# Retention and a two-expert router on one core: short pieces on two column halves, expert 5 turned by transfers, and two constants of the planner

## The chip, the cores and the metric

The kernel runs on one core of a Trainium2 chip. The core has five instruction streams: TensorE (PE, with its weight loads shown apart as PEld), VectorE (DVE), ScalarE (ACT), GpSimd (POOL) and SyncE (SP), and 16 DMA engines that all of them share. SP and POOL issue nearly all transfers. Each stream runs its instructions in the order in which the program has them. The metric is the device time of one execution in microseconds (us). A profiled execution also gives its span, which is the time from its first to its last instruction.

## The reference

Eight batches of 576 tokens go through retention with 8 heads of 64 columns, and the result, as 4608 rows of 512, through a mixture of 8 experts of which each row takes two.

```python
scores = scale * np.matmul(q, k.transpose(0, 1, 3, 2))
Dmat = np.where(rel >= 0, gamma[:, None, None] ** rel[None, :, :], 0.0)
attn = np.matmul(scores * Dmat, v)
x = np.ascontiguousarray(attn.transpose(0, 2, 1, 3)).reshape(B * S, H * D)
...
noisy_logits = x @ w_gate + np.log1p(np.exp(x @ w_noise)) * noise
top2 = np.argpartition(-noisy_logits, 2, axis=1)[:, :2]
top2_w = softmax of the two logits
...
for e in range(8):
    for k in range(2):
        mask = top2[:, k] == e
        h = np.maximum(x[mask] @ w1[e], 0.0)         # 512 -> 1024
        out[mask] += top2_w[mask, k, None] * (h @ w2[e])   # 1024 -> 512
```

The softmax line is told in words; the other lines are the reference's, shortened.

## The kernel before

**Planner.** The kernel first records its operations (`Plan.op`), each with an engine or a choice of engines, a cost, a priority, the buffers that it reads and writes and, for transfers, the DMA time `dma`. `Plan.run` then takes the operations one by one, always the one that can start first by its own bookkeeping, and writes them out in that order. So the costs decide nothing but order, the choice between two engines, and buffer numbers; what waits for what on the chip follows from the data. SP's and POOL's transfers have a lane each, in which a transfer may not be planned ahead of the eighth before it. A POOL transfer was counted as `dma / 0.85`, and one over 2 (the casting weight transfers, 2.9) also pushed back the finish of SP's last eight.

**First stage.** Retention works in 16 units: a pair of batches (`bp`, four of them), four of the eight heads (`hq`), one batch of the pair. Per unit SP loads k, q and v (`load`), the values are scaled and cast to bf16 (`cast`, on ACT, DVE or POOL), PE transposes K and Q (`tr`, line 482) and forms the masked scores (`scores`, 507), the states (`states`, 540) and the output (`out_`, 575 and 585). The last 64 tokens of a batch go through `tail`. The attention's PE work is done on parts of the array: the trace names the part, for example 64\*64 or 128\*64 (rows\*columns). After four units, `route` does a batch pair: logits, the two largest, ranks within each expert (`ranks`, 752 and 754), a table of row numbers by expert (`table`, 805), and the rows themselves, transposed back (828), evicted into `xg` buffers (276 on ACT, 278 on DVE), joined with their weights (834 on POOL) and written to DRAM as `xd` (837 on SP). The room for these rows is ten `xg` buffers, so a pair's rows wait until those of the pair before have landed in `xd`.

**Experts.** An expert has up to 1216 rows, in ten pieces: nine of 128 rows and one of 64, the short piece (`size`). A tile is two to four pieces of one expert (`tiles`), 29 tiles in all, numbered t0 to t28. t0 to t8 belong to experts 0 to 2 and take rows that were routed by the first three batch pairs; they run between and behind the attention's work (`up`, line 1037, then `down`, 1114). The other twenty, from t9 on, go one after another: `wide` (1063) multiplies by `w1`, 32 matmuls per tile with as many columns as the tile has rows, and PE interleaves them with the second multiplication (`second`, 1114) of the tile before, eight matmuls of 128x512 per piece. For a short piece the same eight matmuls are used, and 64 of the 128 result rows are ignored. The very last tile's second multiplication stands alone at the end of `record` (planned at line 1247; its matmuls show as 1114).

Rows are fetched two tiles ahead by gathers on POOL (`fetch`, 961), at the pace of PE: each waits for a matmul that the plan had just emitted. Then they are turned: by PE (983) and an eviction for experts 0 to 5, by transposing transfers on SP (973) for experts 6 and 7 (`CROSS = 6`). A piece in which both kinds of choices meet needs four small operations on DVE (1001 to 1007, `gm` and `im`), which wait for the gather.

Weights of experts 0 to 2 come by casting transfers on POOL (894, 898: four transfers of 512 KB each for an expert), planned behind the loads of units 10, 15 and 15 (`WAIT`). The others come by SP (908, 911) and are cast by ACT and DVE (276, 278), when the tile that frees their room begins.

**Results.** `finish` scales a piece's result by its weight. For a row's first expert it goes to DRAM as `yd` (1148 or 1150, then 1154 on SP). For its second expert `prev` gathers the first result from `yd` (1129 on POOL), DVE joins both (1158), and POOL scatters the rows to the output (1162). Near the end POOL gets a drain (1250), planned behind the first scatter of the last tile but two. After the planned part a loop for overflowing experts (line 1263) runs zero times here.

The functions that the change touches, with the lines of the profile:

Of the kernel before, what the change touches and what calls it, by code (L numbers as in the profile page):

```python
# [10 lines left out]
BF16 = mybir.dt.bfloat16  # L11
# [19 lines left out]
WAIT = (10, 15, 15)  # L31
CROSS = 6
# [7 lines left out]
HD = 64  # L40
C9 = 9
# [14 lines left out]
class Plan:  # L56
# [55 lines left out]
    def run(self):  # L112
# [35 lines left out]
        while ready:  # L148
            pick = None
            for o in ready:  # L150
# [22 lines left out]
                for e, c in o.eng.items():  # L173
# [3 lines left out]
                    if o.dma and len(lanes[e]) >= 8:  # L177
                        t = max(t, lanes[e][-8].fin)
# [20 lines left out]
            if o.dma:  # L199
# [42 lines left out]
class Kernel:  # L242
# [807 lines left out]
    def wide(self, i, t, prio, g2=None):  # L1050
# [5 lines left out]
        for f in range(KF):  # L1056
            p = self.psum("exp")

            def pe(_, f=f, p=p):
# [21 lines left out]
    def down(self, i, t):  # L1081
# [6 lines left out]
        part = lambda g: [divmod(x, KF) for x in range(g * m, g * m + m)]  # L1088

        class Down:  # L1090
# [5 lines left out]
            @staticmethod  # L1096
            def deps(g):
                return ([(hT[f // (KF // len(hT))], f if len(hT) == 4 else f // 2) for s, f in part(g)] +
                        [(w, KD + f // 2) for s, f in part(g)], [po[s] for s in sorted({s for s, f in part(g)})],
                        0.216 * m)  # L1100

            @staticmethod
            def ends(g):
                return [s for s, f in part(g) if f == KF - 1]
# [3 lines left out]
    def second(self, e, po, hT, c, f):  # L1108

# [5 lines left out]
                                        start=(f == 0), stop=(f == KF - 1))  # L1115

# [17 lines left out]
    def finish(self, i, t, s, prio):  # L1134
# [8 lines left out]
        if k != "S":  # L1143
            y = pl.buf("half", "exp")

            def ev(eng, y=y, po=po, g=g, n=n):
                if eng == "ACT":
                    nc.scalar.activation(y.t[:n], po.t[:n], Act.Copy, scale=g()[:n])  # L1148
                else:
                    nc.vector.tensor_scalar(y.t[:n], po.t[:n], g()[:n], None, Alu.mult)  # L1150
            pl.op({"ACT": 0.69, "DVE": 0.7}, 0, ev, r=[po] + src, w=[y], prio=prio)
# [4 lines left out]
        if k != "F":  # L1156
            o, b = pl.buf("half", "exp"), d["prv"][s]
            pl.op("DVE", 0.75, lambda _, o=o, b=b, po=po, g=g, n=n: nc.vector.scalar_tensor_tensor(  # L1158
                o.t[:n], po.t[:n], g()[:n], b.t[:n], Alu.mult, Alu.add), r=[po, b] + src, w=[o], prio=prio)
# [12 lines left out]
    def record(self):  # L1172
# [42 lines left out]
        for i, t in enumerate(ts[:ne]):  # L1215
# [6 lines left out]
            for k in range(KF):  # L1222
                r, w, c = g.deps(k)
                pl.op("PE", c, lambda _, g=g, k=k: [0 for _ in g(k)], r=r, w=w, prio=pr)
# [187 lines left out]
```

## Time and profile before

| what | value |
|---|---|
| median of three runs | 440.3 us (438.19 to 440.85) |
| the profiled execution | 441.0 us, span 439.4 us |
| granted TensorE clock, mean | 0.954 |
| PE, PEld busy | 385.7 us (88%), 245.4 us (56%) |
| DVE, ACT, POOL busy | 179.7 (41%), 240.0 (55%), 286.3 us (65%) |
| second multiplications (1114) | 608 matmuls of 128x512, 202.8 us |
| first multiplications of the wide tiles (1063) | 636 matmuls, 189.0 us |
| PE transposes of gathered rows (983) | 216 of 128x128, 15.4 us |
| transposing transfers on SP (973) | 20, median 4.5 us to landing |
| casting weight transfers on POOL | 12 of 512 KB, median 10.5 us to landing |

The busy share of PE is a mean over two stages. Up to about 186 us the attention, the routing and the first nine tiles share all engines; from there to 431.6 us the wide tiles run. Matmuls overlap in the pipeline, so the mean duration of one (383 ns for 128x512) is longer than its distance to the next. In a row of the windows the columns are: stretch, its length, then busy time and instructions of PE, PEld, DVE, ACT and POOL, then the mean granted clock, the share of the DMA engines' time and GB/s. In a row of the timeline they are: start, duration, engine, line, operation, tiles, form and count, and in brackets how long the engine sat idle before it and what ended that. The form named is that of the first instruction of the row.

### The profile page before, as it was taken

Reading aid. Unit: us, or ns where it says so; the run is one execution under the profiler, and the core shown is the slowest. Engines: PE = TensorE matmul, PEld = TensorE weight load, DVE = VectorE, ACT = ScalarE, POOL = GpSimd, SP = SyncE. Lnnn points to the kernel's source line nnn. Section 1 sums busy time; section 2 is a strip of 40 time slices with the busy share of each in tenths; the row PEclk is TensorE's granted clock in tenths of the full one; section 3 lists DMA queues with packets and bytes.
Section 4 is the critical chain, followed back from the end, with each engine's and each line's share of the span. In section 5 each row is a group of like instructions: output and inputs, shape, how many; then the busy total and the mean of one; then the engine's idle time right before and its main releaser. Section 6 shows DMA issues by size and latency. Waiting matters only on the chain. (4 is left out here: it accounts for less than half of the span.)

```text
span 439.4 us, 11080 instructions
## 1 busy us (share of the span) xinstructions
PE 385.7 (88%) x4252; PEld 245.4 (56%) x4288; DVE 179.7 (41%) x489; ACT 240.0 (55%) x398; POOL 286.3 (65%) x355
## 2 busy tenths in 40 slices
PE   1787884889898959899979999999999999999992
PEld 1665774777676746575545545555454454454451
DVE  2544388778378278213043334026025031131221
ACT  3589693866787436466554747446536524424320
POOL 8875678997789337553446566566577677567344
PEclk9999597969899969999999999999999999999998
DMA  7999999999999988448399897895799997645323
GB/s 193 276 309 233 291 240 310 318 212 247 314 263 196 227 168 242 118 137 297 116 325 387 261 382 236 276 383 167 251 352 278 292 212 224 187 157 174 121 78 140
DMA packets 102489, 105.34 MB, mean 240 GB/s; under 512 B 31870, under 2 KB 80511, under 8 KB 102434
## 3 DMA queue, kind: packets, MB, share of 16 engines
q1 hardware_dynamic: 87170, 67.72, 51.3%
q0 software_dynamic: 15264, 36.89, 32.7%
q8 instruction: 34, 0.56, 0.5%
q14 instruction: 21, 0.17, 0.1%
HBM read 83.20 MB, written 26.63 MB: 250 GB/s over the span
## 5 line engine op out<-in xcount | busy, mean ns | idle before, releaser
L1114 PE MATMUL ps<-W,half 128*128 128x512 bf16 x608 | 202.8, 383 | 0.7 <-issue 0.2
L1063 PE MATMUL ps<-big,W 128*128 128x512 bf16 (+4 forms) x636 | 189.0, 330 | 4.0 <-DVE half L1048 2.8
L1046 ACT ACTIVATE half<-ps 128x512 bf16<-128x512 f32 (+5 forms) x179 | 90.2, 506 | 117.6 <-PE ps L1063 100.7
L961 POOL DMA_INDIRECT xg<-xd,xi x80 | 83.1, 1039 | 64.6 <-ACT half L1046 20.5
L1114 PEld LDWEIGHTS <-half 128*128 128x128 bf16 x640 | 62.6, 99 | 72.6 <-issue 5.6
L1063 PEld LDWEIGHTS <-W 128*128 128x128 bf16 x640 | 63.0, 98 | 47.6 <-issue 0.3
L1158 DVE SCALAR_TENSOR_TENSOR half<-ps,xg,half 128x512 f32<-128x512 f32 (+1 forms) x39 | 29.2, 749 | 79.9 <-PE ps L1114 68.6
L1162 POOL DMA_INDIRECT out_dram<-half,xg x39 | 38.8, 995 | 26.3 <-issue 12.5
L515 DVE TENSOR_TENSOR half<-ps,mask 128x512 bf16<-128x512 f32 x64 | 40.0, 683 | 20.2 <-PE ps L507 20.0
L1129 POOL DMA_INDIRECT half<-yd,xg x39 | 39.4, 1011 | 11.9 <-issue 10.4
L276 ACT ACTIVATE half<-ps 128x1024 bf16<-128x1024 bf16 (+1 forms) x33 | 32.7, 1010 | 12.1 <-PE ps L482 9.4
L482 PE MATMUL ps<-ident__69,half 128*128 128x128 bf16 x256 | 23.8, 251 | 16.6 <-ACT half L449 9.1
L457 POOL TENSOR_TENSOR half<-big,tab 128x1024 bf16<-128x1024 f32 x15 | 28.6, 1904 | 10.3 <-DMA big<-in_q_dram 10.3
L1037 PE MATMUL ps<-half,W 128*128 128x256 bf16 (+1 forms) x288 | 29.8, 260 | 4.5 <-ACT half L276 2.8
L464 POOL TENSOR_TENSOR half<-big,tab 128x512 bf16<-128x512 f32 x32 | 33.0, 1046 | 0.0
L1148 ACT ACTIVATE half<-ps,xg 128x512 f32<-128x512 f32 (+1 forms) x32 | 21.8, 685 | 16.1 <-PE ps L1114 15.8
L482 PEld LDWEIGHTS <-half 128*128 128x128 bf16 x256 | 18.6, 114 | 19.5 <-ACT half L449 9.6
L1037 PEld LDWEIGHTS <-W 128*128 128x128 bf16 x288 | 24.6, 100 | 8.2 <-issue 3.8
L276 ACT ACTIVATE tb<-ps 64x512 bf16<-64x512 f32 x32 | 18.9, 590 | 13.5 <-PE ps L540 13.3
L276 ACT ACTIVATE W<-big 128x1024 bf16<-128x1024 f32 x21 | 21.4, 1055 | 5.7 <-DMA big<-in_moe_w_dram 5.5
L276 ACT ACTIVATE xT<-ps 128x512 bf16<-128x512 f32 (+1 forms) x40 | 19.9, 556 | 7.2 <-PE ps L656 5.0
L1158 DVE SCALAR_TENSOR_TENSOR half<-ps,gm,half 128x512 f32<-128x512 f32 x6 | 4.5, 751 | 46.9 <-ACT half L1148 39.8
(170 smaller groups left out, 415.7 us busy)
## 6 DMA issues: line engine op xcount, KB each, us to landing
big<-in_moe_w_dram SPq DMA_DIRECT2D x40, 512.0 KB, 8.9
yd<-half SPq DMA_DIRECT2D x41, 256.0 KB, 5.2
big<-in_k_dram SPq DMA_DIRECT2D x32, 256.0 KB, 6.1
big<-in_q_dram SPq DMA_DIRECT2D x16, 512.0 KB, 6.0
big<-in_v_dram SPq DMA_DIRECT2D x32, 256.0 KB, 6.3
W<-in_moe_w_dram POOLq DMA_DIRECT2D x12, 512.0 KB, 10.5
xd<-xg SPq DMA_DIRECT2D x16, 264.0 KB, 5.0
xg<-xd,xi POOLq DMA_INDIRECT x80, 4.4
```

Source lines behind the costliest of these rows:

```text
L276: self.nc.scalar.activation(out, in_, Act.Copy)
L464: self.eng(e).tensor_tensor(o, i, t, Alu.mult)
L482: nc.tensor.transpose(v[:, hp, x, :], i[:, y, hp * P:(hp + 1) * P], ident.t)
L515: nc.vector.tensor_tensor(S.t.bitcast(BF16).rearrange("p (h c x) -> p h c x", h=2, c=2)[:, h], p[h].t.rearrange("p (c x) -> p c x", c=2), ...
L961: ins = nc.gpsimd.indirect_dma_start(out=x.t[:n, :], out_offset=None, in_=self.xd[:rows, :], in_offset=IOff(ap=xi.t[:n, h:h + 1], axis=0), ...
L1037: nc.tensor.matmul(pv()[:, f2, :], lhsT=w.t[:, o:o + P], rhs=xv()[:, di, :n], start=(di == 0), stop=(di == KD - 1))
L1046: self.nc.scalar.activation(o, i, Act.Relu)
L1063: self.mm = nc.tensor.matmul(p.t[:, :n], lhsT=w.t[:, o:o + P], rhs=xv()[:, di, :n], start=(di == 0), stop=(di == KD - 1))
L1114: self.mm = self.nc.tensor.matmul(po.t, lhsT=hv[:, c:c + P], rhs=self.W[e].t[:, o:o + DM], start=(f == 0), stop=(f == KF - 1))
L1129: pl.op("POOL", 1.3, lambda _, b=b, iy=iy, n=self.size(j): nc.gpsimd.indirect_dma_start(out=b.t[:n, :], out_offset=None, in_=self.yd[:rows ...
L1158: pl.op("DVE", 0.75, lambda _, o=o, b=b, po=po, g=g, n=n: nc.vector.scalar_tensor_tensor(o.t[:n], po.t[:n], g()[:n], b.t[:n], Alu.mult, Al ...
L1162: ins = nc.gpsimd.indirect_dma_start(out=self.out[:, :], out_offset=IOff(ap=io()[:n], axis=0), in_=o.t[:n, :], in_offset=None, bounds_chec ...
```

## The change

There are four edits, and what the planner makes of them.

1. **Short pieces.** In `down`, a short piece no longer takes part in the interleaving. Its second multiplication stands by itself behind the last step of the tile that follows, as `halves`: for each of the eight parts of `w2` two matmuls of 256 columns with a 64-column stationary operand, the first into result partitions 0 to 63, the second into 64 to 127. `finish` then evicts the two parts by two instructions (`sums`).
2. **Expert 5** (`CROSS` 6 to 5). Its ten pieces, tiles t20 to t22, are turned by transfers on SP, not by PE.
3. **The planner's lanes.** A POOL transfer is counted as `dma / 0.5`, no longer as `dma / 0.85`, and the push on SP's last eight finishes is gone.
4. **The units behind which weights begin** (`WAIT`): 11, 14, 15, no longer 10, 15, 15.

```diff
-WAIT = (10, 15, 15)
-CROSS = 6
+WAIT = (11, 14, 15)
+CROSS = 5
...
-                        t = max(t, lanes[e][-8].fin)
+                        t = max(t, lanes[e][-8])
...
-                    x += o.dma / 0.85
+                    x += o.dma / 0.5
                     if dma_free.get("SP", 0.0) > t + c:
                         dma_free["SP"] += o.dma
-                        for y in lanes["SP"][-8:] if o.dma > 2 else ():
-                            if y.fin > t + c + self.DMA_LAT:
-                                y.fin += o.dma
...
-                lanes[e].append(o)
+                lanes[e].append(o.fin)
...
                 for _ in it:
                     pass
+                if g2:
+                    g2.rest(f)
...
-        part = lambda g: [divmod(x, KF) for x in range(g * m, g * m + m)]
+        full = [s for s in range(m) if self.size(js[s]) == P]
+        short = [s for s in range(m) if self.size(js[s]) < P]
+        n = len(full)
+        part = lambda g: [(full[x // KF], x % KF) for x in range(g * n, g * n + n)]
+        alone = lambda g: [(s, f) for s in short for f in range(KF)] if g == KF - 1 else []
...
+            def rest(g):
+                for s in short if g == KF - 1 else ():
+                    self.halves(e, po[s], hT, self.off(js)[s])
...
+    def halves(self, e, po, hT, c):
+        k = KF // len(hT)
+        for f in range(KF):
+            hv = hT[f // k].t.bitcast(BF16).rearrange("p (f s) -> p f s", f=k)[:, f % k]
+            o = KD * F + f * DM
+            for y in range(2):
+                self.mm = self.nc.tensor.matmul(po.t[y * HD:(y + 1) * HD, :MIDC], lhsT=hv[:, c:c + HD],
+                                                rhs=self.W[e].t[:, o + y * MIDC:o + (y + 1) * MIDC],
+                                                start=(f == 0), stop=(f == KF - 1), skip_group_check=True)
+    def sums(po, n):
+        return [(slice(0, DM), po.t[:n])] if n == P else [
+            (slice(y * MIDC, (y + 1) * MIDC), po.t[y * HD:(y + 1) * HD, :MIDC]) for y in range(2)]
```

Since the costs changed, the order changed on every engine. Up to about 85 us of the profile the orders are the same. Behind that, these are the moves that the prediction speaks of. On SP, the loads of unit 13 stand ahead of the second pair's row writes (837), which they followed in part, and the loads of unit 14 stand close behind these writes. On POOL, the third and fourth casting transfers of expert 0 come later by some ten instructions; those of expert 1 begin ahead of unit 15's casts, two of expert 2 follow these, then four gathers (t6, t7), the first three small operations of the last routing (731, 744, 760), a third transfer of expert 2, a gather of t8, seven small operations, and the fourth transfer; the four gathers stood behind all of these before. On DVE the third pair's routing up to `MM` stands ahead of unit 14's masks, and the rest of it ahead of unit 15's. On PE t2's first multiplication and the third pair's table stand among unit 15's work, ahead of its tail, and four transposes of t3 to t5 ahead of the last ranks; ten pieces, t9 to t12, are turned in a row ahead of the first wide tile. The gather of t15's second piece follows the fifth group of t10's first multiplications, before the seventh. On SP expert 7's weights stand behind the transposing transfers of t20 to t23. On POOL the drain stands behind the third scatter of tile t26, before it stood behind the second; one scatter of t26, two gathers by `prev` for t28, four scatters of t27 and two of t28 follow it.

More of the change, by code (lines that the diff above doesn't have):

```diff
@@ L40 @@
 HD = 64
+MIDC = DM // 2
 C9 = 9
@@ L1223, in record @@
                 r, w, c = g.deps(k)
-                pl.op("PE", c, lambda _, g=g, k=k: [0 for _ in g(k)], r=r, w=w, prio=pr)
+                pl.op("PE", c, lambda _, g=g, k=k: ([0 for _ in g(k)], g.rest(k)), r=r, w=w, prio=pr)
                 for s in g.ends(k):
@@ L1245, in record, with last @@
                 for s in range(len(po)):
-                    pl.op("PE", 1.74, lambda _, s=s: [self.second(e, po[s], hT, self.off(ts[-1][1])[s], f) for f in range(KF)],
+                    def last(_, s=s):
+                        c = self.off(ts[-1][1])[s]
+                        if self.size(ts[-1][1][s]) < P:
+                            self.halves(e, po[s], hT, c)
+                        else:
+                            for f in range(KF):
+                                self.second(e, po[s], hT, c, f)
+                    pl.op("PE", 1.74 if self.size(ts[-1][1][s]) == P else 0.95, last,
                           r=[(hT[f // 2], f) for f in range(KF)] + [(self.W[e], KD + f) for f in range(4)], w=[po[s]], prio=pr)
```

27 lines of the change are left out of this document (16 added, 11 removed).

## The prediction

> **What bounds the kernel now.** The page's slices first, then the windows of the second half, then PE's waits.
>
> ```profile
> span 439.4 us, 11080 instructions
> ...
> PE   1787884889898959899979999999999999999992
> ...
> DMA  7999999999999988448399897895799997645323
> ```
> ```profile
> 186.00:225.00 39.00, 38.03 (x294) 23.89 (x298) 6.59 (x18) 23.64 (x39) 17.79 (x19) 1.00 0.64 195
> 225.00:235.00 10.00, 7.21 (x37) 4.19 (x38) 3.70 (x12) 4.62 (x8) 4.92 (x5) 0.83 1.01 378
> 235.00:431.60 196.60, 195.45 (x1082) 100.62 (x1102) 56.04 (x91) 92.53 (x165) 125.45 (x124) 1.00 0.77 242
> ```
> ```profile
> PE ps L752 <- DVE MM L724: 6.7, 2, 4.4
> ...
> PE ps L983 <- DMA xg<-xd,xi: 0.6, 1, 0.6
> ```
>
> A slice is 11 us. From the seventeenth on PE is full but for one; ahead of that it has holes, while the DMA engines stand at 8 or 9 nearly all the time. So two stages have different limits. From 235 to 431.6 PE is 99.4% busy at full clock: there only less PE work, or a new wait, moves anything. At 225 to 235 stands one hole. In the first stage PE's longest wait is for the routing (L752). The chain that ended last holds only the last transfer and tells nothing; the timeline shows that the tail hangs on POOL:
>
> ```profile
> 411.74 0.75 DVE L1158 SCALAR_TENSOR_TENSOR half<-ps,xg,half 128x512 f32<-128x512 f32 x1 [2.70 <-PE ps L1114]
> 415.19 0.75 DVE L1158 SCALAR_TENSOR_TENSOR half<-ps,xg,half 128x512 f32<-128x512 f32 x1 [2.70 <-PE ps L1114]
> 413.29 0.99 POOL L1162 DMA_INDIRECT out_dram<-half,xg  x1 [2.96 <-issue]
> 421.95 0.98 POOL L1162 DMA_INDIRECT out_dram<-half,xg  x1 [7.67 <-DVE half L1158]
> 433.57 0.99 POOL L1162 DMA_INDIRECT out_dram<-half,xg  x1 [0.30 <-POOLq L1263]
> 427.77 3.83 PE L1114 MATMUL ps<-W,half 128*128 128x512 bf16 x17
> L1250 POOLq DRAIN  x1: 8001/8001/8001, 413.1 to 413.1; - x1
> ```
>
> PE ends at 431.60. POOL's drain holds its queue to 421.1, and then ten transfers follow, 1.29 us apart without a gap (from 421.95 to 433.57 are nine steps), to 434.56.
>
> **Part 1, short pieces: -4.5 us.** Each expert's last piece has 64 rows. A matmul of 512 columns costs (3.83 - 0.38)/16 = 0.2156 us (the L1114 row, its last one's latency taken off), eight of them 1.72. They become eight pairs of 256 columns, one on each column half. Whether pairs run side by side, the attention shows:
>
> ```profile
> 129.98 0.65 PE L540 MATMUL ps<-half,half 128*64 128x192 bf16 x16
> 130.56 0.44 PE L540 MATMUL ps<-half,half 64*64 64x64 bf16 x16
> ...
> 126.60 1.04 PE L1037 MATMUL ps<-half,W 128*128 128x256 bf16 x8
> 127.57 0.64 PE L507 MATMUL ps<-half,half 64*64 64x128 bf16 x32
> 128.14 1.05 PE L1037 MATMUL ps<-half,W 128*128 128x256 bf16 x8
> ```
>
> The first row holds eight matmuls of 192 and eight of 64 columns on half the array's columns: 2048 columns, 0.86 us one after another at 0.421 ns each. The next row starts after 0.58: two at a time (0.43) and a change of shape. What a change costs: the first L1037 row's 8 x 256 columns take 0.86 and L507 starts after 0.97, so 0.11 going in; 32 x 128 columns, four at a time, take 0.43 and the next row starts after 0.57, so at most 0.14 going out. A short piece then costs 8 x 0.108 + 0.21 = 1.07 and saves 0.65. Seven of the eight stand ahead of the tail: 4.5. The eighth ends PE earlier behind POOL's ten transfers and counts nothing. The pieces' evictions become two instructions each on ACT and DVE, busy for less than half of the time from 235 on; if that cover were gone, each would cost one more start, some tenths of a us.
>
> The Trainium skill, TensorEngine Tiling (Array Packing), Key Properties, speaks against this: changing the tiling mode drains TensorE. The trace agrees that it costs something, the 0.11 and 0.14 above. If such a drain laid bare the latency of the last full matmul too (0.38 less 0.22 of columns, on each side), a piece would save 0.33 and the part 2.3.
>
> **Part 2, expert 5 by transfers: -2.1 us.**
>
> ```profile
> 221.51 1.50 PE L983 MATMUL ps<-ident__69,xg 128*128 128x128 bf16 x24
> 222.85 0.54 PE L1063 MATMUL ps<-big,W 128*128 128x192 bf16 x2
> L973 SPq DMA_TRANSPOSE big<-xg x20: 1172/1224/1697, 333.7 to 376.0; - x20
> ```
>
> 24 transposes move the next start by 1.34 us, 56 ns each; 36 full ones and 4 of half the size go, 2.1 us of PE, and with them five evictions. SP gets ten issues of 1.22 us, and expert 7's weights and some rows of y queue behind them, each behind a transfer that waits for its gather. No engine waited for any of the twenty such transfers before, and the new ones stand as far ahead of their tiles; so nothing, and at worst their own issue time for a tile, 4.9.
>
> **Part 3, order of the wide stage: -4.0 us (0 to -5.2, or +2.5), and +1.0.** The hole at 225:
>
> ```profile
> 218.04 2.06 SPq L911 DMA_DIRECT2D big<-in_moe_w_dram  x4
> 215.93 0.99 POOL L961 DMA_INDIRECT xg<-xd,xi  x1 [0.52 <-ACT half L1046]
> 218.96 1.00 POOL L961 DMA_INDIRECT xg<-xd,xi  x1 [2.03 <-ACT half L1046]
> 226.91 0.16 DVE L1001 TENSOR_TENSOR gm<-xg 128x1 f32<-128x1 f32 x1 [4.27 <-DMA xg<-xd,xi]
> 227.79 0.24 PE L1063 MATMUL ps<-big,W 128*128 128x192 bf16 x1 [2.82 <-DVE half L1048]
> ```
>
> DVE waited for one gather (218.96), issued after weight loads (218.04) had begun and landing 7.9 us later; PE's evictions queued behind it on DVE. The clock in that window, 0.83 over 10 us, is 1.7 more; with 0.65 of wait for another gather (the L983 row) the hole is worth 5.2. In the changed order this gather takes the place that the one before it has now, 215.93, ahead of the loads. But DVE's wait also moves, ahead of an eviction of transposes; if the gather is late nevertheless, the hole grows by up to 2.5. I take -4.0, near the whole, since the place of the gather is what the rows show to matter. On the other side ten pieces are now turned in one row ahead of the first wide tile, with two PSUM buffers for them; PE turns two in 0.45, an eviction takes 0.69 (DVE's copy, below) or more: about 1 us of wait, an estimate.
>
> **Part 4, the first stage: -4 us (-10 to +6).** What it offers:
>
> ```profile
> 100.00:120.00 20.00, 17.81 (x350) 13.62 (x342) 11.73 (x23) 14.54 (x23) 15.13 (x20) 0.91 1.04 282
> 155.00:170.00 15.00, 9.66 (x78) 7.47 (x80) 12.81 (x59) 8.02 (x16) 7.80 (x20) 0.77 0.77 165
> 141.64 3.14 SPq L837 DMA_DIRECT2D xd<-xg  x5
> DMA to landing us min/median/max: 14.3/14.3/14.3
> 154.59 0.69 DVE L278 COPY xg<-ps 128x1024 bf16<-128x1024 bf16 x1 [4.69 <-DMA xd<-xg]
> 157.70 0.25 POOL L731 TENSOR_TENSOR d<-bm,am 128x9 f32<-128x9 f32 x1 [10.99 <-DVE bm L708]
> 159.10 0.28 PE L752 MATMUL ps<-MM,ltri 128*128 128x144 bf16 x1 [4.35 <-DVE MM L724]
> 161.03 0.81 POOL L898 DMA_DIRECT2D W<-in_moe_w_dram  x1
> ```
>
> The third batch pair's rows went out from 141.64, among casting weight transfers, and took 14.3 us to land. DVE waited 4.69 for that room with the last routing behind it, and PE got that routing's matrix at 159.10. PE's idle time in 155 to 170 is 5.3, and the clock adds some 2.4; 100 to 120 offers 2.2 and 1.8 in the same way: about 12 in all. In the changed order unit 13's loads stand ahead of SP's wait for routed rows, expert 1's casting transfers come earlier, the third pair's routing stands ahead of unit 15's masks on DVE, and one transfer of expert 2 is taken out of the crowd. So the third pair's rows should go out some 5 us earlier and the last routing should start sooner. Against it: the last quarter of expert 2's weights still goes out behind the last routing's arithmetic, as at 161.03, while PE comes to it sooner; I expect 2 to 4 us of wait there, and other holes that only move. Of 12 I take 4.
>
> **Part 5, the tail: +2.2 us.** The drain now stands behind the third scatter of the last tile but two, not the second. That one waits for DVE's row at 415.19, not 411.74, 3.45 later, and one transfer fewer follows the drain: 3.45 - 1.29. PE's end does not reach it.
>
> **Sum.** -4.5 - 2.1 - 4.0 + 1.0 - 4.0 + 2.2 = -11.4. The profiled execution took 441.0 (span 439.4 and 1.6 around it), so 429.6; the median of the three runs is 0.7 lower, so **429**. The casting factor, the lane rule and the three units cost nothing themselves; they act by the order alone.
>
> **Rivals.** *The first stage only moves its holes*: no part 4, 433. For it: the DMA row is at 8 or 9 throughout, and an order moves no byte fewer. *The halves don't overlap* in this use: 16 x 0.108 + 0.21 is 0.2 more than now for a piece, part 1 turns from -4.5 to +1.5, 435. Against it stands the L540 row. *The first stage gains nearly all* of its 12: 421. *Slower*: four gathers (tiles 6 and 7) now stand on POOL ahead of the last routing's small operations and of expert 2's last two weight transfers, and they need the third pair's rows landed. With the landing of before, 156, they hold POOL to 161 at 1.29 each instead of leaving it free at 157.70, and two more transfers of 1.29 and 0.81 stand ahead of the last quarter, which goes out 6 to 7 us late; PE has no other work there by then. Without parts 3's gain and 4's: 441 - 4.5 - 2.1 + 1.0 + 2.2 + 6.5 = 444, and a us more for each us of later landing. It turns slower from a landing after about 153; I expect 147 to 150.
>
> **Chances.** Forecast 0.50 (424 to 434), holes moved 0.17, no overlap 0.07, nearly all 0.15, slower 0.11. The range takes the forecast, the cases at 433 and 435 with some room, and about half of the one at 421: 420 to 439. Within 1% of 440.3 (435.9 to 444.7) is what a measurement of this kernel can't tell from no change. Of the cases at 433 and 435 a fifth lands there, of the slower one under half: faster 0.80, same 0.11, slower 0.09.
>
> **What would show it.** Part 1: 128 matmuls of 128*64 with 256 columns, a piece's in about 0.87, under 0.3 around them. Part 2: 40 matmuls fewer at L983, no wait of PE for expert 5's tiles. Part 3: no wait of DVE's gm for a gather near 225. Part 4: the third pair's rows landing in under 9 us and the last ranks before 156. Part 5: nine transfers behind the drain, and PE done 4 to 6 us before the last of them. The forecast is wrong if PE waits for weights of expert 1 or 2 for more than 4 us, or if an eviction on DVE again stands behind a late gather.

## The result and the profile after

The changed kernel is **slightly slower**: 445.9 us median of six runs (442.1 to 456.8) beside 439.4 for the kernel before (436.8 to 440.9). The ratio is 1.0116, 95% interval [1.0076, 1.0157], so the loss is clear of zero and under 2%. The forecast was 429, a gain of 2.6%.

The profiled execution of the changed kernel (451.7) is one of its two longest runs, which the ratio leaves out, so the account uses a later execution of 445.8, from a session whose six runs go from 436.8 to 454.6. The runs were taken in several sessions: in some the kernel before takes 440, in others 459. Whether the chip or something else makes this is not shown; the record gives chip 0 for one session of each sort. Ratios are always to the kernel before in the same session; in a session of 459 the changed kernel was equal to it (1.0012 [0.9972, 1.0052]).

The first lines of the page of the 451.7 execution, in 40 slices of 11 us, and then the same lines of the execution of 445.8:

```profile
span 450.0 us, 11154 instructions
...
PE   1686785788888877999998799999999996969991
...
PEclk9999796889999998999999999999999999889996
```
```profile
span 444.1 us, 11189 instructions
...
PE   1687885887978867999998699999999999999991
...
PEclk9999687889999998999999899999999999999996
```

In the kernel before, PE stood at 9 from slice 22 (231) to its end. Now both executions have a hole in slices 22 and 23 (233 to 259), and the long one has two more in slices 34 and 36 (371 to 405), with the clock's digit at 8 in slices 35 and 36. What PE waited for between 186 and 440, first in the kernel before, then in the changed one at 445.8, then in the long execution:

```profile
PE ps L1063 <- DVE half L1048: 2.8, 1, 2.8
PE ps L983 <- DMA xg<-xd,xi: 0.6, 1, 0.6
```
```profile
PE ps L1060 <- DVE half L1045: 3.5, 1, 3.5
PE ps L980 <- DVE half L1184: 1.7, 1, 1.7
PE ps L1122 <- ACT half L1043: 1.5, 1, 1.5
PE ps L1060 <- ACT half L1043: 1.1, 1, 1.1
PE ps L1060 <- ACT big L273: 0.9, 1, 0.9
```
```profile
PE ps L1060 <- ACT half L1043: 4.8, 2, 4.4
PE ps L1122 <- DVE half L1184: 4.3, 1, 4.3
PE ps L1060 <- DVE half L1045: 3.0, 1, 3.0
```

L1060 of the changed kernel is `wide` (1063 before), L1122 `second`, L1043 and L1045 are the evictions of `wide` on ACT and DVE. L1184 is the operation on DVE that joins a row's two results, and L273 an eviction of transposed rows on ACT. Four smaller waits of the long execution (0.5 to 0.8 each) are not shown. So the waits of PE for evictions and joins grew from 2.8 to 8.7 in the execution of 445.8, and to 14.9 in the long one.

Where the time went, by the start of the first `wide` matmul of a tile in each trace (kernel before 439.4 span, changed kernel 444.1):

| stretch | before | changed | difference | forecast for it |
|---|---|---|---|---|
| start to t10 | 207.44 | 210.51 | +3.1 | part 4: -4; part 3: +1 |
| t10 to t13 (holds the hole at 225) | 35.47 | 33.74 | -1.7 | part 3: -4; two short pieces: -1.3 |
| t13 to t14 | 10.53 | 14.98 | +4.5 | 0 |
| t14 to t20 | 73.16 | 69.70 | -3.5 | two short pieces, 40 transposes: -3.4 |
| t20 to t28 | 91.84 | 92.65 | +0.8 | three short pieces: -2.0 |
| t28 to PE's end | 13.16 | 12.54 | -0.6 | 0 (the eighth short piece, not counted) |
| PE's end to the end | 7.81 | 9.94 | +2.1 | part 5: +2.2 |
| all | 439.41 | 444.06 | +4.65 | -11.4 |

Two rows came as worked out (t14 to t20, and the tail). Four others carry the error: the first stage, a new hole between t13 and t14, less from the old hole, and a stretch from t20 to t28 in which the saved PE work is lost again.

**The new hole.** DVE in the changed kernel from 242 to 254 (start, duration, engine, line, operation, output and input; in brackets the idle time before and what ended it), then SP's and POOL's issues before it, then PE:

```profile
251.80 0.16 DVE L998 TENSOR_TENSOR gm<-xg 128x1 f32<-128x1 f32 x1 [4.29 <-DMA xg<-xd,xi]
252.38 1.29 DVE L1045 TENSOR_SCALAR half<-ps 128x320 bf16<-128x320 f32 x3
```
```profile
235.01 11.43 SPq L908 DMA_DIRECT2D big<-in_moe_w_dram  x4
```
```profile
245.15 1.12 POOL L958 DMA_INDIRECT xg<-xd,xi  x1 [0.30 <-issue]
```
```profile
252.93 0.42 PE L1060 MATMUL ps<-big,W 128*128 128x320 bf16 x1 [3.53 <-DVE half L1045]
```

It is the hole of 225 over again, one expert later: a gather is issued (245.15) behind weight loads (235.01 on), lands 6.6 us later, DVE's small operations for the mixed weights (`gm`, L998) wait for it, and three evictions of t13 stand behind them on DVE. PE waits 3.53, and its next matmuls run at half clock (252.7 to 256.1 in the trace). At 225 no evictions stand behind a waiting gather any more: that hole shrank to 0.9.

The old hole gave less than forecast for a reason of the same kind. From t11 to t12 the changed kernel takes 10.70 instead of 13.81, but from t12 to t13 11.33 instead of 9.54. There a join on DVE stood idle for a gather of earlier rows, and PE's transposes waited for that join:

```profile
242.78 0.75 DVE L1184 SCALAR_TENSOR_TENSOR half<-ps,gm,half 128x512 f32<-128x512 f32 x1 [11.17 <-DMA half<-yd,im]
```
```profile
243.58 0.83 PE L980 MATMUL ps<-ident__69,xg 64*128 64x64 bf16 x12 [1.69 <-DVE half L1184]
```

### The profile page after: what moved, and what is told of

Same layout as the page of the kernel before. It is cut to its first block, busy times and chain, and to the rows that moved or that the text cites. A ratio compares the mean times of both kernels' runs of the same rounds, so it can differ in the third digit from the quotient of the medians.

```text
span 450.0 us, 11154 instructions
## 1 busy us (share of the span) xinstructions
PE 377.4 (84%) x4277; PEld 239.2 (53%) x4312; DVE 178.6 (40%) x490; ACT 239.4 (53%) x400; POOL 287.5 (64%) x355
## 5 line engine op out<-in xcount | busy, mean ns | idle before, releaser
L1060 PE MATMUL ps<-big,W 128*128 128x512 bf16 (+4 forms) x633 | 180.8, 331 | 10.4 <-ACT half L1043 4.8
L1122 PE MATMUL ps<-W,half 128*128 128x512 bf16 x548 | 181.5, 384 | 7.6 <-DVE half L1184 4.3
L1043 ACT ACTIVATE half<-ps 128x512 bf16<-128x512 f32 (+5 forms) x181 | 89.4, 508 | 116.3 <-PE ps L1060 85.2
L1122 PEld LDWEIGHTS <-half 128*128 128x128 bf16 x576 | 56.3, 99 | 75.2 <-issue 13.4
L1060 PEld LDWEIGHTS <-W 128*128 128x128 bf16 x640 | 63.0, 99 | 53.6 <-issue 7.7
L1184 DVE SCALAR_TENSOR_TENSOR half<-ps,xg,half 128x512 f32<-128x512 f32 (+1 forms) x46 | 30.2, 667 | 77.4 <-PE ps L1122 32.9
L273 ACT ACTIVATE half<-ps 128x1024 bf16<-128x1024 bf16 (+1 forms) x34 | 34.0, 1014 | 19.9 <-PE ps L479 12.8
L273 ACT ACTIVATE W<-big 128x1024 bf16<-128x1024 f32 x21 | 22.1, 1054 | 16.1 <-DMA big<-in_moe_w_dram 13.8
L1174 ACT ACTIVATE half<-ps,xg 128x512 f32<-128x512 f32 x33 | 22.5, 685 | 15.2 <-PE ps L1122 14.6
L479 PEld LDWEIGHTS <-half 128*128 128x128 bf16 x256 | 18.6, 115 | 20.8 <-POOL half L454 10.9
L273 ACT ACTIVATE tb<-ps 64x512 bf16<-64x512 f32 x32 | 18.9, 590 | 11.5 <-PE ps L537 10.8
L1184 DVE SCALAR_TENSOR_TENSOR half<-ps,gm,half 128x512 f32<-128x512 f32 x6 | 4.5, 751 | 51.0 <-ACT half L1174 40.2
L273 ACT ACTIVATE xT<-ps 128x512 bf16<-128x512 f32 (+1 forms) x40 | 19.9, 556 | 5.1 <-PE ps L653 3.0
```

What stands on the lines that cost most here:

```text
L273: self.nc.scalar.activation(out, in_, Act.Copy)
L479: nc.tensor.transpose(v[:, hp, x, :], i[:, y, hp * P:(hp + 1) * P], ident.t)
L1043: self.nc.scalar.activation(o, i, Act.Relu)
L1060: self.mm = nc.tensor.matmul(p.t[:, :n], lhsT=w.t[:, o:o + P], rhs=xv()[:, di, :n], start=(di == 0), stop=(di == KD - 1))
L1122: self.mm = self.nc.tensor.matmul(po.t, lhsT=hv[:, c:c + P], rhs=self.W[e].t[:, o:o + DM], start=(f == 0), stop=(f == KF - 1))
L1184: pl.op("DVE", 0.75 if n == P else 0.86, lambda _, o=o, b=b, po=po, g=g, n=n: [nc.vector.scalar_tensor_tensor(o.t[:n, c], x, g()[:n], b.t[ ...
```

## The experiments

One table first; the ratio is to the kernel before in the same session, with its interval. Where the interval reaches beyond 2%, or holds one, the size of the effect is open.

| run | edit | kernel before in that session | ratio |
|---|---|---|---|
| e1 | changed, CROSS = 6 | 440.7 | 1.010 [1.006, 1.015] |
| e2 | before, CROSS = 5 | 440.7 | 1.015 [1.006, 1.023] |
| e3 | before, short pieces | 440.7 | 0.987 [0.976, 0.997] |
| e4 | before, short pieces, CROSS = 5 | 440.7 | 0.988 [0.979, 0.997] |
| e5 | e3, `gm` late | 459.2 | 0.996 [0.990, 1.002] |
| e6 | changed, `gm` late | 459.2 | 0.987 [0.980, 0.993] |
| e7 | e3, WAIT | 459.2 | 1.019 [1.008, 1.030] |
| e8 | e3, casting factor and lane rule | 459.2 | 1.015 [1.008, 1.023] |
| e9 | short pieces, order of before held | 459.6 | 1.000 [0.996, 1.004] |
| e10 | e9, one `gm` moved | 459.6 | 0.999 [0.994, 1.003] |
| e11 | changed, expert 5 not turned | 459.6 | 0.996 [0.991, 1.001] |
| e12 | changed | 459.6 | 1.001 [0.997, 1.005] |
| e13 | before | 459.5 | 1.004 [0.997, 1.010] |
| e14 | e3, drain ahead | 459.5 | 1.002 [0.995, 1.009] |
| e15 | changed, gathers of t6 to t8 later | 459.5 | 0.995 [0.989, 1.002] |
| e16 | changed, drain ahead | 459.5 | 1.011 [0.996, 1.026] |
| e17, e18 | changed with `gm` late; changed | 440.1 | medians 441.1 and 447.4 |

### One part at a time: e1 to e4

```diff
-CROSS = 5
+CROSS = 6          (e1, in the changed kernel; e2 is the reverse, in the kernel before)
```

e3 takes `halves`, `sums`, and the short pieces' planner costs into the kernel before; e4 adds CROSS = 5 to that.

> The changed kernel with expert 5's ten pieces turned by PE again (CROSS back to 6); everything else as changed. Theory A: the ten added transposing transfers crowd the DMA engines in 300 to 400 (in the changed kernel's profile a gather of earlier rows lands 9.4 us after its issue in that stretch, 3.7 before; PE waits 4.4 at 382 and 4.3 at 403, each followed by a stretch at half clock). Then this kernel loses both waits: gathers land in about 4 us in 300 to 400, PE's idle time in 350 to 400 is below 1, and the time is 433 to 437, below both kernels. Theory B (rival): the holes come from the changed order and the short pieces' split evictions, not from the transfers; then the holes stay and the 2.1 us of transposes on PE come back: 445 or more.

> The kernel before with one edit: expert 5's ten pieces turned by transfers (CROSS = 5), with the old planner constants and short pieces of full width. Theory A: the transfers alone crowd the queues; gathers in 300 to 400 take about twice their 3.7 us, PE waits there for evictions that stand behind them, and the time is 442 to 448. Theory B: transfers cost nothing here; 40 transposes fewer on PE give 2 us: 437 to 438.

> The kernel before with one edit: the short pieces as sixteen matmuls on two column halves, with their split evictions and their planner costs; CROSS, WAIT and the casting factor as before. The prediction's part 1: 0.65 us for each of seven pieces, 4.5 in all, so 435. Rival: lone short pieces or split evictions make new waits, so that less than half is left: 437 to 441.

> The kernel before with two of the edits, short pieces on the halves and expert 5 by transfers, without the planner's edits (casting factor, lane rule, WAIT). Theory A: what the transfers cost on the queues outweighs the short pieces' gain, and the wide stage has the waits of the changed kernel near 380 and 400: 439 to 445. If the first stage's new order (the planner's edits) were the loss instead, this would be 432 to 434.

The short pieces alone are faster by 1.3% (forecast: 1.0%). Expert 5 by transfers alone is slower by 1.5%, where the prediction had it gain 0.5%. But with the short pieces it costs nothing (e4 beside e3), and taking it out of the changed kernel (e1) does not mend it: 444.9, where theory A said 433 to 437 and theory B 445 or more. What e1 and the changed kernel share and e3 and e4 do not have is the planner's three edits (casting factor, lane rule, `WAIT`); they go with 1.7% to 2.4%, which is more than the whole loss.

Both theories hold in part, as the traces show. In the sessions of 440 PE waits 4.1 to 9.6 us after 340 in four traces with CROSS = 5 (changed 9.6, e2 4.1, e4 7.2, e17 7.4) and 2.6 in a fifth (e18); in the kernel before it does not wait there. e1 has no wait of this kind but 2.7 at 340 for DVE's copy of pieces that PE had turned, and 4.2 at 248. The transfers' rows, of the kernel before (from 300 to 420), then of the changed kernel (451.7): median from issue to landing is the last number, over those of them whose landing the trace has (4 to 11 of a row).

```profile
half<-yd,xg POOLq DMA_INDIRECT x28, 3.7
...
big<-xg SPq DMA_TRANSPOSE x20, 4.5
xg<-xd,xi POOLq DMA_INDIRECT x19, 4.2
```
```profile
half<-yd,xg POOLq DMA_INDIRECT x28, 9.4
big<-xg SPq DMA_TRANSPOSE x27, 13.4
...
xg<-xd,xi POOLq DMA_INDIRECT x18, 10.3
```

In the execution of 445.8 the rise is smaller: 10.0 for the transposing transfers, 4.6 and 6.5 for the two kinds of gathers. In e2, where `CROSS` is the only edit, it is 8.9, 4.8 and 8.3. One wait on ACT and PE, and SP's issues, in the long execution:

```profile
381.39 1.09 ACT L1043 ACTIVATE half<-ps 128x512 bf16<-128x512 f32 x2 [12.89 <-DMA out_dram<-half,xg]
```
```profile
382.04 0.59 PE L1060 MATMUL ps<-big,W 128*128 128x512 bf16 x1 [4.44 <-ACT half L1043]
```
```profile
349.60 35.11 SPq L970 DMA_TRANSPOSE big<-xg  x12
```

SP took 35 us to issue twelve transposing transfers (1.22 each before), the gathers beside them land later, an eviction on ACT needs a buffer from which a scatter is still reading, and PE stands. With CROSS = 6 and PE faster (e3) the landing of the tiles' gathers also rose, to 9.5, and that of the twenty transposing transfers to 10.6, yet PE waited 1.0 only. So the ten added transfers are not the only load there, and how long PE waits differs from run to run.

### The operations that wait on DVE: e5, e6, e10, e17, e18

In e5, e6 and e17 the four `gm` and `im` operations of an expert are planned behind the last eviction of the wide tile before:

```diff
-                pl.op("DVE", 0.17, lambda ...: V.tensor_tensor(gm.t, ...), r=[x], w=[gm], prio=prio)
+                def mixed(after, ...):
+                    pl.op("DVE", 0.17, lambda ...: V.tensor_tensor(gm.t, ...), r=[x], w=[gm], prio=prio, after=after)
...
+                for x in self.t[i]["late"]:
+                    x(begun)
                 late = i > ne and ts[i - 1][0] < e and any(...)
```

> The kernel before with the short pieces, and with the four small operations that make an expert's mixed weights and offsets (they wait on DVE for a gather) planned behind the last eviction of the wide tile before, not at the gather. Theory C: each such wait is a wait of PE only because evictions of the wide multiplication stand behind it on DVE. Then the wait of 4.74 at 226 in the kernel with short pieces alone goes, with the 3.4 us at half clock that follow it (1.7): 437.5 - 6.4 = 431. Rival: PE is held by the weights or the gathered rows themselves at that place, and the wait stays under another name: 436 to 439.

> The changed kernel with the same four operations planned behind the last eviction of the wide tile before. Theory C: the wait of 3.0 to 4.2 near 249 goes, and the half clock behind it where there was one (2 to 3 us): 446 - 3 to 6, so 440 to 443, and the rest of the loss (first stage, crowded transfers, tail) stays. Rival: the wait moves to another place again: 444 to 447.

> The changed kernel with the mixed expert's small operations planned behind the last eviction of the wide tile before, run beside the changed kernel on one chip. On another chip it was 1.3% under the kernel before, where the changed kernel (in other runs) was equal to it. Theory C, that DVE's wait for a late gather ahead of evictions is worth one hole with its half clock: 0.7 to 1.4% under the changed kernel, wherever it runs. Rival, that the order only shifts holes: within 0.4% of it.

> The changed kernel itself beside it. On the first chip it was 1.2% slower than before, on a slower one equal: if that is the chip, a chip where before takes about 440 shows 1.0 to 1.4% again, one where it takes 459 shows 0.

e17 and e18 ran beside each other. Sorted, the six runs of e17 are 430.1, 436.6, 436.7, 445.5, 446.6, 448.9, those of the changed kernel 436.8, 445.8, 447.1, 447.8, 453.1, 454.6; each is lower by 2.3 to 10.3, the medians by 6.3 (1.4%, the upper end of what was expected). Both spread too far for an interval, and the changed kernel's median lies 1.7% over the kernel before, where 1.0 to 1.4% was expected. In the traces t13 to t14 takes 11.40 instead of 14.98, and t13's evictions on DVE stand behind no gather:

```profile
245.29 0.49 DVE L1050 TENSOR_SCALAR half<-ps 128x320 bf16<-128x320 f32 x1
246.34 0.49 DVE L1050 TENSOR_SCALAR half<-ps 128x320 bf16<-128x320 f32 x1 [0.56 <-PE ps L1065]
```

In a session of 459 e6 is at 0.987 [0.980, 0.993], and in another the changed kernel is at 1.001 [0.997, 1.005]. Theory C stands for the changed kernel, on these two comparisons. For the kernel with short pieces alone (e5) the gain was not there: 0.996 beside an expected 0.980. e10 is the sharpest of these: the order of the kernel before held on every engine, and four instructions moved on DVE behind five evictions, by a step after the planning:

```diff
+        last = [o for o in order if o in self.marks["ev", 11] and o.on == "DVE"][-1]
+        order = self.put(order, self.marks["gm", 3], last)
```

> The same with one more edit: four small operations of expert 3 (they wait on DVE for a gather, at 226.9 in the kernel before) stand behind the five evictions of the 192-column tile that follow them, nothing else moved. Theory C: PE's wait of 2.8 there (and the half clock behind it, 1.7) is made by that place alone: 3 to 5 us less than with the short pieces alone, so 1.7 to 2.1% under the kernel before, and no PE wait near 227. Rival: PE then waits for DVE's later work, or for the weights, and at most 1 us is gained.

DVE without and with this edit (e9, then e10):

```profile
235.79 0.17 DVE L1002 TENSOR_TENSOR gm<-xg 128x1 f32<-128x1 f32 x1 [3.67 <-DMA xg<-xd,xi]
```
```profile
236.81 0.15 DVE L1028 TENSOR_TENSOR gm<-xg 128x1 f32<-128x1 f32 x1
```

The wait is gone, and t11 to t12 takes 9.16 instead of 13.21. But the next two tiles take 2.4 more, by small waits for evictions and one of 2.1 for which the trace names nothing, and the whole execution is at 0.999. Where DVE's wait stood the mechanism is shown; that its 4 us reach the end is not, in that session.

### The planner's edits: e7 and e8

```diff
-WAIT = (10, 15, 15)
+WAIT = (11, 14, 15)                     (e7)
-                    x += o.dma / 0.85   (e8, with the lane rule)
+                    x += o.dma / 0.5
```

> The kernel with short pieces, and of the planner's edits only the units (WAIT = 11, 14, 15); casting factor, lane rule and CROSS as before. The short pieces alone gave 437.5; short pieces with all planner edits and CROSS = 6 gave 444.9. If the units make the first stage longer (t10 2.5 us later there), this kernel is at 440 to 444 and its t10 after 207; if not, 436 to 438.

> The kernel with short pieces, and of the planner's edits only the casting factor (0.5) and the lane rule; units (10, 15, 15) and CROSS = 6. If these two move the waits of the wide stage (the gather behind weight loads from 225 to 249, the copy at 340) and put the drain behind the third scatter, the kernel is at 441 to 445, with a PE wait of 3 to 4 near 249 and 10 us from PE's end to the end; if the units alone do it, 436 to 438.

With either alone the kernel with short pieces is 1.5 to 1.9% slower than the kernel before in the same session, where e5, e9 and e14, which have short pieces without these edits, are at 0.996 to 1.002. The places are others than expected: in e7 PE waits 3.5 for gathered rows at 200, six times 0.6 to 2.1 for more between 230 and 261, and 2.8 at 389; in e8 4.0 at 154, 3.7 at 173, 2.2 and 2.3 at 195 and 198, and 2.3 and 2.4 at 330 and 404. Of what was expected e8 has the 10.7 us from PE's end to the end, but nothing over 1 near 249. So it is not one of the two that carries the loss, and there is no one place: each new order has holes of its own.

### The first stage: e15

```diff
-                   w=[x], prio=prio, dma=0.4, pace=pace, slack=3)
+                   w=[x], prio=prio, dma=0.4, pace=pace, slack=3,
+                   after=self.paid if early == 2 else ())
```

> The changed kernel with the five gathers of tiles 6, 7 and 8 held (in the planner) behind the last routing's small operations on POOL. The prediction's rival of a slower kernel: these gathers hold the last routing, its rows go out 3 us later (171.6 for 168.6) and the wide stage's first gather 4.4 later (180.3 for 175.9). Then the rows go out at 168.5 or sooner, the first gather of the wide stage near 176, t10 starts 2 to 4 earlier than in the changed kernel, and the time is 2 to 4 under it. If PE has enough other work there, t10 stays where it is, within 1.

The prediction's slower rival was here word for word, in the 451.7 execution:

```profile
157.71 1.10 POOL L958 DMA_INDIRECT xg<-xd,xi  x1 [10.57 <-DVE M L713]
...
162.77 0.22 POOL L728 TENSOR_TENSOR d<-bm,am 128x9 f32<-128x9 f32 x1
...
167.66 0.85 POOL L895 DMA_DIRECT2D W<-in_moe_w_dram  x1
```

Four gathers ahead of the last routing's small operations, the last quarter of the weights 6.6 later than the 161.03 of before. With the gathers behind the routing (e15) that quarter goes out at 164.16, but the routed rows still at 171.81 (170.01 in e12, the changed kernel in another session of 459), and t10 starts at 213.69 beside 213.55. The rival's price falls: PE had other work there. e15's median is 4.7 below e12's all the same, in two sessions; the ratios are 0.995 and 1.001, with intervals that overlap. The traces show one place that fits: the order had changed behind that point too, and t13 to t14 takes 10.34 instead of 16.10.

What did hold the first stage? The third pair's routing stands some 9 us earlier on PE, and its rows go out at the same time:

```profile
134.14 0.23 PE L752 MATMUL ps<-MM,ltri 128*128 128x144 bf16 x1
```
```profile
125.06 0.22 PE L749 MATMUL ps<-MM,ltri 128*128 128x144 bf16 x1 [0.66 <-DVE MM L721]
```
```profile
131.49 0.56 POOL L728 TENSOR_TENSOR d<-d,r 128x9 f32<-128x9 f32 x1
...
137.73 0.22 POOL L780 TENSOR_TENSOR py<-py,keep_t 128x9 f32<-128x9 f32 x1
```
```profile
141.15 3.97 SPq L834 DMA_DIRECT2D xd<-xg  x5
```

Between ranks and rows lie 16 us instead of 7.5 (134.14 to the 141.64 of before): the routing's small operations on POOL stand among gathers and casts. So the early start on PE did not bring the rows out earlier, and by 150 PE has done less of its work, 837 matmuls instead of 926 from 100 on (first row before, second row the execution of 445.8):

```profile
100.00:150.00 50.00, 45.65 (x926) 36.17 (x922) 33.16 (x78) 35.64 (x59) 39.77 (x57) 0.97 1.05 251
```
```profile
100.00:150.00 50.00, 41.55 (x837) 32.04 (x834) 32.34 (x75) 36.25 (x59) 40.18 (x58) 1.00 1.08 255
```

Behind that the table of the last routing makes PE wait for DVE, 3.13 in this execution, in the long one and in e1, where the kernel before had no such wait:

```profile
174.53 1.36 PE L802 MATMUL ps<-oh,olo 128*128 128x80 f16 x18 [3.13 <-DVE oh L797]
```

This is read from the traces; no kernel that gives the routing way on POOL there was run, so the cause of the 3.1 us in this stage stays open.

### The tail: e14 and e16

```diff
-        for o, t in order:
+        order = self.put(order, self.marks["drain", 0], self.marks["drain", 1][0])
+        for o in order:
```

> The kernel with short pieces alone (planner and CROSS as before), its order held, with POOL's drain of the tail moved ahead, behind the first scatter of the last tile but two. If the drain sets the tail, PE's end to the end of the span falls from 8.0 to about 4.5, and the kernel is 3 us under the one with short pieces alone: 1.5 to 2.2% under the kernel before. If the last transfers' landing sets it, the tail stays at 7 to 8 and the kernel is at -1.3%.

> The changed kernel, its order held, with POOL's drain of the tail behind the first scatter of the last tile but two instead of the third. The prediction's part 5 (+2.2 for the later drain): PE's end to the end of the span falls from 9.9 to 7 or less, and the time by 2 to 5. If nothing hangs on the drain, it stays at 9 to 10.

Nothing was gained that can be measured. From PE's end to the end it takes 11.5 in e14 and 13.1 in e16, beside 9.7 for the kernel before (e13), 12.2 for e9 and 10.7 for e12, all in sessions of 459. In e16 the drain is over at 433.8, but eleven transfers follow it, two of them gathers of earlier rows that the last tile adds to. Moving the drain ahead leaves all of these behind it; the drain itself keeps its 7.6.

### The short pieces with nothing else, and what stays open: e9, e11 to e13

e9 keeps the kernel before's order on every engine; only the matmuls and the evictions of the short pieces differ.

> The kernel before with its order of instructions held on every engine, and only the short pieces' matmuls replaced by the two halves (alone, behind the step at which the kernel before ended the piece) and their evictions split. This is the prediction's part 1 without any reordering: 0.65 us for each of seven pieces, 4.5 in all, 1.0% under the kernel before. If a lone short piece lays bare a drain on each side (0.33 a piece), 0.5%; if a split eviction makes a new wait, none.

> The kernel before itself, for its trace on the chip of these runs: where this chip is the slower one (about 459 instead of 440), the trace shows which stage holds the 19 us, and what a tile with a short piece takes there, to be set beside the kernel with short pieces in the same order (t14 to t28 took 171.3 in that one).

> The changed kernel with its order held; nine of expert 5's ten transposing transfers are plain transfers of the same bytes, so expert 5's rows reach its matmuls unturned (this leaves out the turning). Theory A: what crowds the queues at 300 to 400 are the many small packets of the transposing transfers; then gathers there land in about 4 us (9.4 in the changed kernel), PE's waits near 382 and 403 go, and the time is 5 to 10 us under the changed kernel. Rival: the order of the transfers on SP makes the waits, whatever their kind; then they stay and the time is that of the changed kernel within 2.

> The changed kernel itself, for comparison on the same chip: 1.0 to 1.5% slower than before, with PE waits of 3 or more near 250 and between 375 and 405.

A piece costs what was worked out. In the changed kernel (451.7), PE around one:

```profile
367.05 0.81 PE L1060 MATMUL ps<-big,W 128*128 128x512 bf16 x3
367.79 1.06 PE L1132 MATMUL ps<-W,half 128*64 128x256 bf16 x16
368.79 0.39 PE L1060 MATMUL ps<-big,W 128*128 128x512 bf16 x1
```

From 367.79 to 368.79 it is 1.00, and three matmuls of 0.216 end at 367.70, so 0.09 more ahead of it: 1.09 for the 1.07 forecast, 0.64 saved. Still e9 is at 1.000 [0.996, 1.004] in a session of 459, where e3 was at 0.987 in one of 440. e13's trace has the kernel before in a session of 459: it loses 10.3 by t9 (207.7 instead of 197.4) and 6.7 between t22 and t23 (16.3 instead of 9.6), and PE's waits in that tile often have no releaser in the trace. Why the 4 us do not reach the end there stays open.

e11 was meant to take the small packets away and did not: the plain transfers too were cut at 256 bytes (17388 packets under 512 bytes in 285 to 420, 17521 in e12). It is 0.5% below e12, and the intervals overlap. Turning as such is not shown to cost anything; whether it is the packets or the number of transfers is open.

## Why the prediction was wrong, by its own steps

The edits taken one at a time (e1 to e4) say which parts failed. The short pieces gave 1.3%, about what was forecast. Expert 5's transfers, worth -2.1 in the sum, made no difference beside the short pieces (e4 and e3, and the changed kernel and e1, differ by about 0.1%) and cost 1.5% without them (e2). The planner's edits, parts 3 to 5 with -4.8 in the sum, go with 1.7 to 2.4% more time, 7 to 11 us. Part 5 came about as forecast, so parts 3 and 4 together, -7.0 in the sum, had the wrong sign, and that is the larger error.

**Part 1, -4.5: right in its mechanism.** A piece took 1.09 for 1.07; 128 matmuls of 128*64 with 256 columns, as said, and in the execution of 445.8 no wait around them in seven of eight. The short pieces alone gave 0.987 in a session of 440; with the order held, in a session of 459, they gave nothing (e9).

**Part 2, -2.1: the step that failed is "No engine waited for any of the twenty such transfers before ... so nothing".** 40 transposes went (180 and 20 at L980 for 216 and 24), and t14 to t20 got its 3.5. But the ten transfers were priced by their issue alone, and not by what they do to transfers beside them. The transposing transfers' own landing rose to 10.0 from 4.5 in the execution of 445.8, the gathers' by 0.9 and 2.3, and all to more than twice in the long one. From t20 on the waits (2.6 and 9.6) took the gain back: t20 to t28 is 2.8 over its forecast. Since e3, without the added transfers, shows late landings too, how much of this is theirs alone is not settled. The bound of 4.9 that I gave was for another wait.

**Part 3, -4.0 and +1.0: the step that failed is "I take -4.0, near the whole, since the place of the gather is what the rows show to matter".** What mattered was the place of DVE's wait in front of evictions. The wait at 225 did go, to 0.9. The same pattern came back at 249, where the order also puts a gather behind weight loads and `gm` ahead of three evictions, for 4.5 us, and in a milder form at 243, for 1.7. I had compared the orders only at the hole that existed. The prediction's own warning, an eviction on DVE again behind a late gather, is what happened. The other term, 1.0 for the ten pieces turned in one row, is part of the first row of the table and cannot be told apart there.

The Trainium skill, TensorE: Matmul & The Clock Gate, section The HAM clock gate, says that an idle window of about 3.4 us makes the clock fall to half. The trace agrees in kind: behind the waits of 3.53 here and of 2.82 in the kernel before, 3.4 us run at half clock. The 2.82 is less than the page's window, and so are 2.24 in e2 (at 226) and 1.98 in e4 (at 390), which had such a stretch behind them. But a wait of 3.02 in the long execution (at 250), of 2.73 in e1 (at 340), and those of 1.69, 1.5 and 1.1 here had none. So in these traces the length of a wait does not decide by itself whether the clock falls.

**Part 4, -4: the step that failed is "the third pair's rows should go out some 5 us earlier".** They went out at 142.55 for 141.64 in the execution of 445.8, and at 141.15 in the long one. The one landing that each trace gives for them is 7.6 and 7.3 instead of 14.3, as promised, but DVE's wait for the room of these rows ended at 157.61 and 155.06 (154.59 before), and the last ranks came at 162.12 and 159.58 (159.10), not before 156. The first stage ended later, by t10's start 3.1 and 1.2. Of the rivals, "only moves its holes" describes it, with the sign still too good.

**Part 5, +2.2: right in its mechanism.** From PE's end it is +2.1, of which 0.6 only stands there because the eighth short piece lets PE end earlier; from t28's start to the end it is +1.5. Nine transfers follow the drain, and PE is done 5.3 us before the last of them.

```profile
419.36 0.98 POOL L1189 DMA_INDIRECT out_dram<-half,xg  x1 [2.47 <-DVE half L1184]
428.07 0.98 POOL L1189 DMA_INDIRECT out_dram<-half,xg  x1 [7.73 <-DVE half L1184]
...
438.41 0.99 POOL L1189 DMA_INDIRECT out_dram<-half,xg  x1 [0.30 <-issue]
```

**The rivals and the chances.** The slower rival had its conditions met and yet not its price (e15); the kernel got slower by another way, and that its 444 lies near the measured 445.9 is luck. Its rows add up to 5.6 for the delay, where it says 6 to 7; the long execution had 6.6. The deeper fault lies in the chances. Three edits of a list scheduler change every order behind 85 us, and I gave them one gain each and a chance of 0.09 to a slower kernel. The runs show what such edits do: e7 and e8 are new orders with holes at other places, 1.5 to 1.9% slower.

**The best kernel.** In a session of 440 the short pieces alone (e3: 437.5 beside 440.7) and with expert 5 by transfers (e4: 438.1) beat both kernels, by few runs; in one of 459 e6 does. No one kernel was shown to be best in both.

## What to carry to other kernels

A change of a planner's constants is to be priced as a new order, not as a list of gains: look in the new order for every place with the pattern of the old hole (an instruction that waits for a transfer, with evictions queued behind it on its engine), not at the old hole alone. Work moved from a full engine to the DMA queues has to be priced by the landing times of the transfers beside it. And an edit that is local, as the short pieces are, is best tried with the order held.

## What was not expected of the hardware

- Sessions differ by more than the change: the same kernel takes 440 in some and 459 in others, and an edit that costs 1% in one sort costs nothing in the other (the changed kernel 1.012 and 1.001). What makes the difference is not known.
- With ten more transposing transfers SP takes longer to issue one. The row of SP for them, of the changed kernel's long execution (least, median and most in ns) from 300 to 420; the kernel before had 1172, 1224 and 1697. In e2, where this is the only edit, the thirty have a median of 1.58 us and at most 5.58; with twenty transfers e1 and e3 have at most 3.4:

```profile
L970 SPq DMA_TRANSPOSE big<-xg x27: 1171/1937/6053, 299.3 to 391.0; - x27
```
